# Attention and a leaky-ReLU feed-forward on one core: order of the last half products, copies of the last range on ScalarE, and no stores by GpSimd

## The chip, the core and the metric

The kernel runs on one core of a Trainium2 chip. A core has TensorE (PE in the profile, with its weight loads as PEld), VectorE (DVE), ScalarE (ACT), GpSimd (POOL) and SyncE (SP), which all run their own instruction streams and wait for one another by semaphores, and 16 DMA engines. The metric is the device time of one execution in microseconds; 387.52 us is the median of three executions of the kernel before (387.19 to 387.84).

## The reference

Softmax attention over 8 batches, 12 heads, 448 positions and 64 values per head, then a feed-forward with leaky ReLU over the 3584 tokens:

```
scores = scale * np.matmul(q, k.transpose(0, 1, 3, 2))
attn = np.exp(scores - max) ; attn = attn / (sum(attn) + 1e-09)
x = np.matmul(attn, v).transpose(0, 2, 1, 3).reshape(3584, 768)
h = x @ w_in                      # 768 -> 2048
g = np.maximum(0.01 * h, h)
return (g @ w_out).astype(np.float32)   # 2048 -> 768
```

## The kernel before

The 3584 tokens are cut into seven ranges (`cuts`); all but the first (640) and the sixth (384) have 512 tokens. After the attention of the first batches, the kernel handles range after range: `hidden(i)` computes the hidden values h of range i, and `second(i)` multiplies them by w_out and stores the result. Between the pieces of `second` a planner (`place`, with modelled times) puts attention work for the later ranges. In the last range no attention is left.

From the second range on, both parts use a scheme with seven products in place of eight for each 2 x 2 arrangement of blocks, at the price of extra sums and differences. In `hidden` these come from `mix_x_part` (line 500, differences of x on VectorE, made ahead of time while the preceding range's output part runs).

In the output part the four blocks of 128 tokens of a range form two pairs, and `block_pair(i, c)` treats one: c = 0, then c = 1. Its products P1 to P7 have 128 tokens, 384 output columns and eight matmuls each (line 679), issued in four pieces of two matmuls; between the pieces the generator yields. P1, P3, P5 accumulate in one PSUM bank (`b`), P2, P4, P6 in the other (`a`). `keep` (line 684) copies a bank into an output tile in SBUF, on VectorE or ScalarE; `join` (line 687, VectorE) adds a bank to what stands there. The two output tiles of a pair are `o1` and `o2`, each of 768 columns in f32, from a pool of three buffers. Lines 691 and 697 are differences of h on VectorE that later products need.

From the second range on, P7 of both pairs together is itself done with seven products of half the depth and half the columns: `deep(i)` (line 644), four matmuls of 192 columns each, here called half products 1 to 7. Half products 1, 3, 5 and 7 go to one bank, 2, 4 and 6 to another, and each is followed by an addition on VectorE (line 645) from the bank into `kept[i, 0]` or `kept[i, 1]`, the tiles o2 of the two pairs. The sums of h that deep needs are made at line 620 (`deep_sums`) and 647. Half product 4 is the first that adds to the second pair's o2, into columns that `keep(o2, left, b)` has filled from P5's bank just before. Half product 6 goes on top of half product 4's bank, half product 7 on top of half product 5's.

In the second pair the half products stand between the pieces of P5 (`fifth`) and P6 (`sixth`): half products 1, 2 and 3 behind the first three pieces of P5; 4, 5 and 6 behind the first three pieces of P6; 7 at the end. In the last range P6 of the second pair is split into two products of 192 columns, each with its own addition (line 733) and store, and half product 4 stands behind the first four of P6's sixteen matmuls, 5 and 6 behind the third and the last four.

`store` (line 399) writes a tile to HBM in two transfers, since 128 tokens touch two strips of the output. All go out on SyncE's queue, except in the last range, where some go out on ScalarE's, and the two of `kept[6, 0]`'s left half on GpSimd's. A store on SyncE or ScalarE waits for its addition and for the transfer that last used its completion semaphore. Line 1230 is the end of the program, where the engines drain and meet.

Of the kernel before, what the change touches and what calls it, by code (L numbers as in the profile page):

```python
# [9 lines left out]
F32 = mybir.dt.float32  # L10
# [6 lines left out]
def kernel(  # L17
# [9 lines left out]
    nc = tc.nc  # L27

    B, H, S, D = q.shape
    DM, DF = moe_w_in.shape  # L30
    P = 128
# [5 lines left out]
    NW = DM // 2  # L37
# [4 lines left out]
    NR = len(cuts) - 1  # L42
# [16 lines left out]
    o_pool = ctx.enter_context(tc.tile_pool(name="o", bufs=3))  # L59
# [9 lines left out]
    def next_slot():  # L69

        slots.append(slots.pop(0))
        return slots[-1]
# [17 lines left out]
    e_all = exp_pool.tile([P, NE, EL + EP], BF16, name="e")  # L90
# [22 lines left out]
    w_out_sb = w_pool.tile([P, MD, DM], BF16)  # L113
    MH = MD // 2
    w_mix = w_pool.tile([P, 3, MH, NW], BF16)
    QH, QW = MH // 2, NW // 2
    deep_mix = w_pool.tile([P, 3, QH, QW], BF16)
    KEEP = 4
    h = h_pool.tile([P, MD, (KEEP + 1) * P], BF16, name="h")
# [270 lines left out]
    def store(o, t0, cols=slice(0, DM), queues=(nc.sync, nc.sync)):  # L390

        queues = list(queues)
        done = 0
        while done < P:
            b, j = divmod(t0 + done, S)
            so, p = divmod(j, SC)
            n = min(SC - p, P - done)
            dst = out[b * S:(b + 1) * S].rearrange("(p so) n -> so p n", so=NSC)
            queues.pop(0).dma_start(out=dst[so, p:p + n, cols], in_=o[done:done + n, cols])  # L399
            done += n  # L400
# [102 lines left out]
    def spots(i):  # L503

        if i == 0:
            return 0, [(0, 1), (2, 3)]
        return 0, [(0, 2), (1, 3)] if cuts[i + 1] - cuts[i] == 4 * P else [(0, 1), (KEEP, 2)]

    def token(i, x):

        return KEEP * P if x == KEEP else cuts[i] + x * P
# [96 lines left out]
    kept = {}  # L608
# [14 lines left out]
    def deep(i):  # L623

        one, two = (ts(x[1], P) for x in spots(i)[1])
        lo, hi = slice(MH, MH + QH), slice(MH + QH, MD)
        s3, s1 = h_mix[:, :QH, 0], h_mix[:, QH:, 0]
        t, (t2, t3, t4) = w_mix[:, 2], (deep_mix[:, x] for x in range(3))
        left, right = slice(0, QW), slice(QW, NW)
        o = [kept[i, c] for c in range(2)]  # L630
        end = i + 1 == NR
        taken = [slots.pop(0) for _ in range(2)]
        b, a = (x[:, 0, :QW] for x in taken)
        for ps, first, x, w, c, cols in (
            (b, True, h[:, lo, one], t[:, :QH, left], 0, left),
            (a, True, h[:, hi, one], t[:, QH:, left], 0, left),
            (b, False, s1, t2, 0, right),
            (a, True, h[:, lo, two], t[:, :QH, right], 1, right),
            (b, False, s3, t3, 1, right),
            (a, False, h[:, hi, one], t[:, QH:, right], 0, right),  # L640
            (b, False, h[:, hi, two], t4, 1, left),
        ):
            for m in range(QH):
                nc.tensor.matmul(ps, x[:, m], w[:, m], start=(first and m == 0), stop=(m == QH - 1), skip_group_check=True)  # L644
            nc.vector.tensor_add(o[c][:, cols], o[c][:, cols], ps)  # L645
            if ps is a and first and c == 0:
                nc.vector.tensor_sub(h[:, hi, one], h[:, hi, one], s1)
            t0 = token(i, spots(i)[1][c][1])
            if ps is a and not first:
                store(o[0], t0, slice(0, NW) if end else slice(0, DM), (nc.gpsimd, nc.gpsimd) if end else (nc.sync, nc.sync))  # L650
            if end and c == 1 and ps is b:
                store(o[1], t0, cols, (nc.sync, nc.scalar))
            yield
        if not end:
            store(o[1], token(i, spots(i)[1][1][1]))
        slots.extend(taken)
        for x in taken:
            model["free"][id(x)] = model["now"] + 1.2

    def block_pair(i, c):  # L660

        lo, hi = slice(0, MH), slice(MH, MD)
        x1, x2 = spots(i)[1][c]
        one, two = ts(x1, P), ts(x2, P)
        s3 = h_mix[:, :, c]
        t2, t3, t4 = (w_mix[:, x] for x in range(3))
        t1 = w_out_sb[:, lo, NW:]
        left, right = slice(0, NW), slice(NW, DM)
        o1 = o_pool.tile([P, DM], F32, name="o")
        o2 = kept[i, c] = o_pool.tile([P, DM], F32, name="o")  # L670
        b, a = banks
        t0 = token(i, x2)
        last = t0 + P == B * S

        def product(ps, x, w, first=False, cols=slice(0, NW)):
            for m in range(MH):
                if m in (2, 4, 6):
                    yield
                nc.tensor.matmul(  # L679
                    ps[:, cols], x[:, m], w[:, m], start=(first and m == 0), stop=(m == MH - 1), skip_group_check=True,  # L680
                )

        def keep(o, at, ps, by=nc.vector.tensor_copy):
            by(o[:, at], ps[:, :NW])  # L684

        def join(o, at, ps):
            nc.vector.tensor_add(o[:, at], o[:, at], ps[:, :NW])  # L687

        yield
        yield from product(b, h[:, lo, one], w_out_sb[:, lo, left], first=True)  # L690
        nc.vector.tensor_sub(h[:, lo, one], h[:, lo, two], h[:, lo, one])
        short = cuts[i + 1] - cuts[i] < 4 * P
        keep(o1, left, b, nc.scalar.copy if c == 0 and (short or i + 1 == NR) else nc.vector.tensor_copy)
        yield
        yield from product(a, h[:, hi, one], w_out_sb[:, hi, left], first=True)
        join(o1, left, a)
        nc.vector.tensor_sub(h[:, hi, one], h[:, hi, one], h[:, lo, one])
        yield
        yield from product(b, h[:, lo, one], t2)
        keep(o1, right, b)  # L700
        yield
        yield from product(a, h[:, lo, two], t1, first=True)
        keep(o2, right, a)
        yield

        def fifth():
            yield from product(b, s3, t3)
            join(o2, right, b)
            if i:
                keep(o2, left, b, nc.scalar.copy if c else nc.vector.tensor_copy)  # L710
                if last:
                    store(o1, token(i, x1), left)
                    store(o2, t0, right, (nc.sync, nc.scalar))
                elif i + 1 == NR:
                    store(o2, t0, right)

        def sixth():
            if not last:
                yield from product(a, h[:, hi, one], w_out_sb[:, hi, right])
                join(o1, right, a)  # L720
                store(o1, token(i, x1))
                return
            for x in range(2):
                cols = ts(x, QW)
                for m in range(MH):
                    if m == QH or x and m == 0:
                        yield
                    nc.tensor.matmul(
                        a[:, cols], h[:, hi, one][:, m], w_out_sb[:, hi, right][:, m, cols], start=False, stop=(m == MH - 1),
                        skip_group_check=True,  # L730
                    )
                at = slice(NW + x * QW, NW + (x + 1) * QW)
                nc.vector.tensor_add(o1[:, at], o1[:, at], a[:, cols])
                store(o1, token(i, x1), at, (nc.sync, nc.scalar))

        if i and c:
            more = deep(i)
            for x, _ in enumerate(fifth()):
                yield
                next(more)  # L740
                yield
            yield
            for x, _ in enumerate(sixth()):
                yield
                if not last or x != 1:
                    next(more)
                    yield
            yield
            for _ in more:
                yield  # L750
            return
        yield from fifth()
        yield
        sums = deep_sums(i) if i else ()
        for _ in sixth():
            next(sums, None) if i else None
            yield
        if i:
            return
        yield  # L760
        yield from product(b, h[:, hi, two], t4)
        keep(o2, left, b)
        store(o2, t0)
        banks.reverse()
# [140 lines left out]
    idle = next_slot()  # L905
    slots.pop()
    a, b = idle[:, 0], idle[:, 1]
# [327 lines left out]
```

## Time and profile before

| | |
|---|---|
| median of three executions | 387.52 us |
| profiled execution: time, and span from first to last instruction | 389.63 us, 387.8 us |
| granted TensorE clock | 0.995 |
| busy: TensorE, VectorE, ScalarE, GpSimd | 96%, 64%, 66%, 47% |
| HBM read and written | 45.61 MB, 11.01 MB |

Rows of the timeline show start, length, engine, line of the kernel, operation, output<-input and how many instructions are merged, and in brackets the idle time of the engine ahead of it and what ended that. TensorE's rows overlap: a matmul's result is finished after the next one has been issued, so the distance between starts is what one costs. An engine name with a q (SPq) is its instruction queue, which issues and waits. Times are microseconds from the start of the span.

### The profile page before, as it was taken

The page shows a single profiled execution, that of the slowest core. Times are in us where ns is not written, and L with a number is a line of the kernel's source. Part 1 is how long each engine was busy: PE and PEld are TensorE (multiplying, and loading weights), DVE is VectorE, ACT ScalarE, POOL GpSimd, SP SyncE. Part 2 cuts the span into 40 slices and gives each one's busy share as a digit, 9 for nine tenths or more (in the row PEclk, how much of TensorE's full clock was granted, in tenths as well). Part 3 has the DMA queues.
Part 4 walks back from the last instruction along what each step waited for, and adds up shares of the span by engine and source line. Part 5 has one row for each costly group of instructions (what it writes and reads, how often), then busy time and mean ns, then how long its engine had stood idle before and what let it go on. Part 6 is the DMA issues. An engine that isn't in the chain of part 4 may idle for free.

```text
span 387.8 us, 10131 instructions
## 1 busy us (share of the span) xinstructions
PE 372.3 (96%) x4016; PEld 265.9 (69%) x4016; DVE 247.3 (64%) x551; ACT 257.8 (66%) x397; POOL 181.6 (47%) x378
## 2 busy tenths in 40 slices
PE   7899999989999999999999999999999999999992
PEld 3565657756598556986569865688666986688762
DVE  4763838455766867666666666666666675775772
ACT  5998885764858875488764887647876488338400
POOL 8998720977969656741558405584045100000001
PEclk9999999999999999999999999999999999999998
DMA  9999999799999759891599914999148600330022
GB/s 156 200 201 204 167 174 197 88 144 216 152 118 188 101 119 177 168 125 29 107 150 206 125 27 88 162 201 138 27 88 148 164 2 12 80 111 13 1 83 82
DMA packets 99536, 47.85 MB, mean 123 GB/s; under 512 B 63728, under 2 KB 96240, under 8 KB 99488
## 3 DMA queue, kind: packets, MB, share of 16 engines
q0 software_dynamic: 40464, 22.67, 47.6%
q1 hardware_dynamic: 58448, 24.07, 32.4%
q8 instruction: 31, 0.51, 0.5%
q10 hardware_dynamic: 576, 0.47, 0.4%
q14 instruction: 17, 0.14, 0.1%
HBM read 45.61 MB, written 11.01 MB: 146 GB/s over the span
## 4 chain that ended last, share of the span: by engine, by line
PE 72%; DMA 15%; DVE 6%; issue 3%; POOL 2%; ACT 1%; POOLq 0%; DVEq 0%; ACTq 0%
PE g L679 23%; PE g L553 13%; PE sc L553 13%; DMA fk<-in_k_dram 11%; PE sc L319 6%; PE sc L347 6%; DMA qkT<-qkb 2%; PE sc L340 2%; DMA w_in_mix<-in_k_dram 2%; PE sc L316 2%; PE sc L644 2%; DVE o L645 2%; PE g L359 1%; PE g L777 1%; PE sc L359 1%
## 5 line engine op out<-in xcount | busy, mean ns | idle before, releaser
L328 ACT ACTIVATE e<-sc 128x896 bf16<-128x896 f32 (+1 forms) x144 | 123.5, 921 | 35.6 <-PE sc L319 20.8
L679 PE MATMUL g<-w_out_sb,h 128*128 128x384 bf16 x408 | 80.7, 326 | 0.2 <-DVE o L687 0.2
L679 PEld LDWEIGHTS <-h 128*128 128x128 bf16 x520 | 48.3, 98 | 36.9 <-issue 10.0
L186 POOL COPY qkb<-fq 112x512 bf16<-112x512 bf16 x36 | 23.9, 665 | 92.7 <-DMA qkT<-qkb 73.4
L542 ACT ACTIVATE h<-c 128x512 bf16<-128x512 f32 (+1 forms) x72 | 43.5, 611 | 24.8 <-DVE c L568 15.4
L553 PEld LDWEIGHTS <-w_in_sb 128*128 128x128 bf16 x576 | 54.3, 98 | 5.3
L553 PEld LDWEIGHTS <-w_in_mix 128*128 128x128 bf16 x432 | 41.2, 98 | 4.1
L976 DVE RECIPROCAL rec<-sc 112x8 f32<-112x8 f32 x42 | 8.7, 207 | 43.4 <-PE sc L347 22.5
L399 POOL DMA_DIRECT2D out_dram<-o x2 | 1.1, 546 | 73.7 <-DVE o L645 73.7
L347 PE MATMUL sc<-v,e 128*128 128x65 bf16 x720 | 33.3, 193 | 0.0
L319 PE MATMUL sc<-qkT 64*128 64x448 bf16 (+1 forms) x210 | 32.8, 352 | 0.0
L684 DVE COPY o<-g 128x384 f32<-128x384 f32 x44 | 24.3, 552 | 12.2 <-PE g L679 11.8
L347 PEld LDWEIGHTS <-e 128*128 128x128 bf16 x720 | 31.1, 98 | 1.3
L977 DVE TENSOR_TENSOR x<-sc,rec 112x512 bf16<-112x512 f32 x42 | 29.0, 691 | 1.7 <-DVE rec L976 0.2
L687 DVE TENSOR_TENSOR o<-o,g 128x384 f32<-128x384 f32 x38 | 20.9, 550 | 12.2 <-PE g L679 10.6
L553 PE MATMUL sc<-xT,w_in_sb 128*128 128x256 bf16 (+1 forms) x216 | 28.5, 268 | 0.0
L553 PE MATMUL g<-xT,w_in_sb 128*128 128x256 bf16 (+1 forms) x216 | 28.5, 268 | 0.0
L340 PE MATMUL sc<-v,e 128*128 128x130 bf16 x120 | 26.5, 221 | 0.0
L684 ACT COPY o<-g 128x384 f32<-128x384 f32 x8 | 3.8, 478 | 33.2 <-DVE o L687 27.0
L679 PE MATMUL g<-w_mix,hmix 128*128 128x384 bf16 x104 | 23.0, 327 | 0.0
L316 PE MATMUL sc<-qkT 64*128 64x448 bf16 x144 | 19.5, 354 | 3.3 <-DMA qkT<-qkb 1.4
L159 POOL DMA_DIRECT2D fv<-in_v_dram x33 | 20.6, 631 | 4.1 <-POOL v L199 2.4
(144 smaller groups left out, 770.4 us busy)
## 6 DMA issues: line engine op xcount, KB each, us to landing
fq<-in_q_dram POOLq DMA_DIRECT2D x18, 224.0 KB, 6.2
w_in_sb<-in_moe_w_in_dram POOLq DMA_DIRECT2D x4, 768.0 KB, 10.8
w_out_sb<-in_moe_w_out_dram POOLq DMA_DIRECT2D x4, 768.0 KB, 20.4
out_dram<-o SPq DMA_DIRECT2D x7, 336.0 KB, 3.4
out_dram<-o SPq DMA_DIRECT2D x7, 288.0 KB, 2.7
fk<-in_k_dram POOLq DMA_DIRECT2D x15, 128.0 KB, 6.1
fv<-in_v_dram POOLq DMA_DIRECT2D x15, 128.0 KB, 5.8
out_dram<-o SPq DMA_DIRECT2D x7, 240.0 KB, 4.2
```

What stands on the lines that cost most here:

```text
L186: by(t[:SC, x].rearrange("p so h d -> p h so d"), f)
L316: nc.tensor.matmul(ps[:, j, :S], t[p, S + c * SC:S + c * SC + P], t[p, :S], start=True, stop=True)
L319: nc.tensor.matmul(ps[:, j, :S].rearrange("p (so s) -> p so s", so=NSC), t[p, 1, c], t[p, 0, :, :SC], start=True, stop=True,)
L328: nc.scalar.activation(e[:, :, c, :], ps[:n, :, :S], AX.Exp, scale=scale)
L340: nc.tensor.matmul(ps, e[:, EM + qc * SC:EM + qc * SC + P], vt[:, 2 * KC:].rearrange("p j d -> p (j d)"), start=True, stop=False, skip_gro ...
L347: nc.tensor.matmul(ps[:, j * (D + 1):(j + 1) * (D + 1)], e[:, at:at + P], vt[:, j * KC + c], start=False, stop=(c == KC - 1), skip_group_c ...
L542: nc.scalar.activation(hs[:, m:m + 2, cols], x.rearrange("p (m t) -> p m t", m=2), AX.Prelu, alpha=0.01)
L553: nc.tensor.matmul(ps[:, j * nh:(j + 1) * nh], w[:, kk, ts(j, P)], x[:, kk], start=(first and j == 0 and kk == 0), stop=(kk == KH - 1), sk ...
L679: nc.tensor.matmul(ps[:, cols], x[:, m], w[:, m], start=(first and m == 0), stop=(m == MH - 1), skip_group_check=True,)
L684: by(o[:, at], ps[:, :NW])
L687: nc.vector.tensor_add(o[:, at], o[:, at], ps[:, :NW])
L977: nc.vector.tensor_mul(x, ps[:, :, :, :D], rec.to_broadcast([SC, 2, 2 * NP, D]))
```

## The change

The half products are moved: in the second pair of each range from the second on but the last, half product 4 comes behind the second piece of P6 instead of the first, 5 behind the third, and 6 and 7 after all of P6. In `fifth`, the copy of P5's bank into the left half of o2 now stands ahead of the join of that bank, and VectorE does it for both pairs (before, ScalarE did it for the second pair, behind the join). In the last range P6 of the second pair is one product of 384 columns with one join and one store in two transfers; half product 4 comes behind its first piece, 5 behind its third, 6 and 7 after it. In that range the copies of P1, P3 and P4 are ScalarE's (before, only P1's of the first pair), the second pair's tiles o1 and o2 are parts of the attention buffer `e_all` instead of pool buffers, and the stores of `kept[6, 0]`'s left half go out on SyncE and ScalarE instead of GpSimd.

```
@@ deep
             if ps is a and not first:
-                store(o[0], t0, slice(0, NW) if end else slice(0, DM), (nc.gpsimd, nc.gpsimd) if end else (nc.sync, nc.sync))
+                store(o[0], t0, slice(0, NW) if end else slice(0, DM), (nc.sync, nc.scalar if end else nc.sync))
@@ block_pair
-        o1 = o_pool.tile([P, DM], F32, name="o")
-        o2 = kept[i, c] = o_pool.tile([P, DM], F32, name="o")
+        if i + 1 == NR and c:
+            o1, o2 = (e_all[:, x, :2 * DM].bitcast(F32) for x in range(2))
+        else:
+            o1, o2 = (o_pool.tile([P, DM], F32, name="o") for _ in range(2))
+        kept[i, c] = o2
...
+        idle = nc.scalar.copy
+        calm = idle if i + 1 == NR else nc.vector.tensor_copy
...
-        keep(o1, left, b, nc.scalar.copy if c == 0 and (short or i + 1 == NR) else nc.vector.tensor_copy)
+        keep(o1, left, b, idle if c == 0 and short else calm)
...
-        keep(o1, right, b)
+        keep(o1, right, b, calm)
...
-        keep(o2, right, a)
+        keep(o2, right, a, calm)
...
         def fifth():
             yield from product(b, s3, t3)
+            if i:
+                keep(o2, left, b)
             join(o2, right, b)
             if i:
-                keep(o2, left, b, nc.scalar.copy if c else nc.vector.tensor_copy)
                 if last:
...
         def sixth():
-            if not last:
-                yield from product(a, h[:, hi, one], w_out_sb[:, hi, right])
-                join(o1, right, a)
-                store(o1, token(i, x1))
-                return
-            for x in range(2):
-                cols = ts(x, QW)
-                for m in range(MH):
-                    if m == QH or x and m == 0:
-                        yield
-                    nc.tensor.matmul(
-                        a[:, cols], h[:, hi, one][:, m], w_out_sb[:, hi, right][:, m, cols], start=False, stop=(m == MH - 1),
-                        skip_group_check=True,
-                    )
-                at = slice(NW + x * QW, NW + (x + 1) * QW)
-                nc.vector.tensor_add(o1[:, at], o1[:, at], a[:, cols])
-                store(o1, token(i, x1), at, (nc.sync, nc.scalar))
+            yield from product(a, h[:, hi, one], w_out_sb[:, hi, right])
+            join(o1, right, a)
+            store(o1, token(i, x1), right if last else slice(0, DM), (nc.sync, nc.scalar if last else nc.sync))

         if i and c:
             more = deep(i)
-            for x, _ in enumerate(fifth()):
+            for _ in fifth():
                 yield
                 next(more)
                 yield
             yield
             for x, _ in enumerate(sixth()):
                 yield
-                if not last or x != 1:
+                if x != int(last):
                     next(more)
                     yield
-            yield
             for _ in more:
                 yield
             return
```

The attention work that the planner puts between the pieces stands at the same places in the changed program.

## The prediction

> **What bounds the kernel now.** I read the busy shares first, then a table by stage, then the waits, then the places where TensorE (PE) waits, and last the end of the program.
>
> ```profile
> PE 372.3 (96%) x4016; PEld 265.9 (69%) x4016; DVE 247.3 (64%) x551; ACT 257.8 (66%) x397; POOL 181.6 (47%) x378
> ```
>
> ```profile
> 362.50:382.20 19.70, 18.24 (x132) 12.06 (x130) 14.00 (x31) 1.93 (x4) 0.06 (x1) 1.00 0.20 57
> 382.20:387.80 5.60, 0.00 (x0) 0.00 (x0) 0.00 (x0) 0.00 (x0) 1.01 (x2) 0.68 0.28 85
> ```
>
> The columns are window, length, then busy time of PE, PEld, VectorE (DVE), ScalarE (ACT) and GpSimd (POOL), granted clock, DMA share, GB/s. Over the whole run TensorE is busy 96%. In the output part of the last range (362.5 to 382.2) it loses 1.5 us, and then 5.6 us pass with no arithmetic at all. TensorE therefore sets the time up to about 382, and whatever ends last after it sets the rest.
>
> ```profile
> DVE o L645 <- ACT o L684: 2.4, 5, 0.6
> PE sc L644 <- DVE o L645: 2.4, 4, 0.9
> SPq L1230 <- PEq L1230: 2.1, 2, 1.6
> ```
>
> These rows of the table of waits (who <- for whom: total, times, longest) name the two places the change touches: a chain ScalarE copy -> VectorE addition -> sixth half product, and a wait of SyncE's queue at the closing line 1230. Below, "half products" 1 to 7 are those of the function deep, P1 to P7 those of the pair, and "middle ranges" are the five from the second to the sixth.
>
> **Middle ranges: what is removed and what comes instead.** PE, VectorE and ScalarE rows of the third range (202 to 205 us), then of the second (153 to 156), then of the sixth (341 to 344):
>
> ```profile
> 202.20 0.54 DVE L687 TENSOR_TENSOR o<-o,g 128x384 f32<-128x384 f32 x1
> ...
> 202.66 0.49 PE L679 MATMUL g<-w_out_sb,h 128*128 128x384 bf16 x2
> 202.82 0.48 ACT L684 COPY o<-g 128x384 f32<-128x384 f32 x1 [2.50 <-issue]
> 203.34 0.81 DVE L645 TENSOR_TENSOR o<-o,sc 128x192 f32<-128x192 f32 x2 [0.59 <-ACT o L684]
> 203.74 0.49 PE L644 MATMUL sc<-w_mix,h 128*128 128x192 bf16 x4 [0.59 <-DVE o L645]
> ...
> 204.39 0.49 PE L644 MATMUL sc<-deep_mix,h 128*128 128x192 bf16 x4
> ...
> 204.72 0.49 PE L553 MATMUL g<-xT,w_in_sb 128*128 128x256 bf16 x3
> ```
>
> ```profile
> 153.84 0.68 DVE L500 TENSOR_TENSOR x_mix<-xT 128x512 bf16<-128x512 bf16 x1
> 154.50 0.35 DVE L645 TENSOR_TENSOR o<-o,sc 128x192 f32<-128x192 f32 x1
> ...
> 155.11 0.35 DVE L645 TENSOR_TENSOR o<-o,sc 128x192 f32<-128x192 f32 x1
> ```
>
> ```profile
> 155.89 0.82 PE L553 MATMUL g<-xT,w_in_sb 128*128 128x256 bf16 x6
> ```
>
> ```profile
> 341.49 0.55 DVE L687 TENSOR_TENSOR o<-o,g 128x384 f32<-128x384 f32 x1
> 341.96 0.42 DVE L500 TENSOR_TENSOR x_mix<-xT 128x512 bf16<-128x512 bf16 x1
> 342.59 0.35 DVE L645 TENSOR_TENSOR o<-o,sc 128x192 f32<-128x192 f32 x1 [0.21 <-ACT o L684]
> 342.86 0.42 DVE L500 TENSOR_TENSOR xT<-xT 128x512 bf16<-128x512 bf16 x1
> 343.20 0.35 DVE L645 TENSOR_TENSOR o<-o,sc 128x192 f32<-128x192 f32 x1
> ```
>
> ```profile
> 342.60 0.49 PE L679 MATMUL g<-w_out_sb,h 128*128 128x384 bf16 x2
> ...
> 343.98 0.82 PE L553 MATMUL g<-xT,w_in_sb 128*128 128x256 bf16 x6
> ```
>
> Third range, before: the fifth product's sum is joined by VectorE at 202.20, copied by ScalarE at 202.82, and only then can the addition of half product 4 run (203.34), because it adds to columns that the copy writes. Half product 6 writes the bank that this addition reads, so TensorE starts it at 203.74 instead of right behind the piece at 202.66. A piece or half product takes 0.33 us of issue (204.39 to 204.72).
>
> Third range, after: VectorE copies at 202.20 and joins one step later. Two neighbouring VectorE operations of this size stand 0.47 us apart (341.49 to 341.96), so the join is at 202.67 and the addition of half product 4 at 203.14, 0.20 earlier. TensorE followed the start of that addition by 0.40 (203.34 to 203.74, 0.05 behind its end), so half product 6 starts at 203.54. All four pieces of P6 now stand ahead of it, so only one half product follows it, not a piece and a half product. The addition of half product 5, 0.46 behind that of 4 (0.81 for the two less 0.35), ends at 203.95 and frees the bank of half product 7, which starts at 204.00 and ends its issue at 204.33, against 204.72 before: a gain of 0.39. The addition may also have to wait for the whole join (0.54 and not 0.47): then 0.3. The fourth and fifth range have the same order on VectorE; I take 0.33 for each of the three, together 1.0.
>
> Second range: there VectorE has work on x_mix (L500, 0.68) between the join and the addition, and ScalarE's copy was hidden under it. The copy on VectorE pushes everything back by 0.47: additions at 154.97 and 155.58, the latter ending at 155.93, half product 7 at 155.98, next stage at 156.31 against 155.89. A loss of 0.42. Sixth range: additions at 342.76 (one x_mix step of 0.33 behind the join) and 343.36, the latter ending at 343.71. TensorE's own order would bring half product 7 to 343.58 (342.60 plus three steps of 0.33); it starts at 343.76 and the next stage at 344.09, a loss of 0.11.
>
> Sum of the middle ranges: 1.0 - 0.42 - 0.11 = a gain of 0.4 to 0.5; I take **0.4**. Bounds: if the copy cost its whole 0.47 in the three ranges too, less the piece of 0.33 that is moved, the five would lose 0.95; if no stall were left at all, they would gain the 2.4 of the table. The nearest rows are those above, so I keep 1.0 of loss and 1.2 of gain for the range.
>
> At no cost: the changed order of copy and join in the first pair of each range (both are VectorE's already, and the last of the two ends at the same time); the stores of a middle range, two of which swap on SyncE's queue (the buffers are written again only after the next range's hidden stage, for instance 343.98 to 362.49 on TensorE); ScalarE's copy, 0.48, which nothing waits for any more. VectorE's x_mix work ends up to 0.47 later; TensorE needs it some two steps into the hidden stage, and without that cover each such stage would lose up to 0.47.
>
> **Last range: products and additions.** The same chain and a split P6:
>
> ```profile
> 378.20 0.55 DVE L687 TENSOR_TENSOR o<-o,g 128x384 f32<-128x384 f32 x1
> ...
> 378.66 0.49 PE L728 MATMUL g<-w_out_sb,h 128*128 128x192 bf16 x4
> ...
> 379.97 0.49 PE L728 MATMUL g<-w_out_sb,h 128*128 128x192 bf16 x4 [0.82 <-DVE o L733]
> ...
> 381.49 0.68 DVE L645 TENSOR_TENSOR o<-o,sc 128x192 f32<-128x192 f32 x2
> 382.14 1.08 POOL L399 DMA_DIRECT2D out_dram<-o  x2 [73.73 <-DVE o L645]
> ```
>
> P6's second half waits until its first half has been read out (379.97). After the change P6 is one product of full width, with the same TensorE time (16 matmuls of 192 columns were four steps, 8 of 384 are four). P6 begins at 378.00 (two steps of 0.33 ahead of the row at 378.66), and from there TensorE runs eight steps without that stop: half product 5 at 379.31, 6 at 379.97, 7 at 380.30, each done 0.49 after its start, the last at 380.79. On VectorE: copy 378.20, join 378.67, additions of 4 at 379.14 and of 5 at 379.84 (when half product 5 is done), join of P6 at 380.17, additions of 6 at 380.64 and of 7 at 380.97, ending at 381.32 against 382.17: **0.85 earlier**. The copies moved to ScalarE (five in the two pairs) take 0.48 there, as at 202.82, and each has one product into the other bank, four steps or 1.3 us, to hide under; without that cover TensorE would stop up to 0.5 each time. New waits: the joins of this range wait for ScalarE's copies, which end some 0.8 ahead of them (1.3 less 0.48); behind a join stand the sums of h and the additions, for which TensorE waits. The two output tiles taken from the attention buffers are free: their last readers ran at 335.
>
> ```profile
> L340 PE MATMUL sc<-v,e x120: 219/220/231, 107.7 to 335.2; 128*128 128x130 bf16 x120
> ```
>
> **Last range: stores and the end.**
>
> ```profile
> 381.72 0.88 ACTq L399 DMA_DIRECT2D out_dram<-o  x2
> ```
>
> ```profile
> L1230 SPq EVENT_SEMAPHORE  x11: 17/28/28, 385.0 to 387.8; - x11
> ...
> L1230 POOLq DRAIN  x3: 46/102/4437, 382.6 to 387.6; - x3
> L1230 SPq DRAIN  x3: 7/7/7, 385.6 to 387.3; - x3
> ```
>
> ```profile
> out_dram<-o ACTq DMA_DIRECT2D x1, 168.0 KB, 2.3
> out_dram<-o ACTq DMA_DIRECT2D x2, 84.0 KB, 2.0
> out_dram<-o SPq DMA_DIRECT2D x1, 144.0 KB, 2.7
> ...
> out_dram<-o POOLq DMA_DIRECT2D x1, 144.0 KB, 2.4
> ```
>
> The closing code (line 1230; columns: count, shortest/median/longest in ns, first and last start) shows what stands at the end. GpSimd issues its second store at about 382.7 (two in 1.08 from 382.14) and it lands 2.3 to 2.4 later, at 385.0, where SyncE's last waits go through; at 385.6 they are done. Then SyncE stands 1.6 more (the longest wait in its row above), and the only thing still running is GpSimd's drain: 4.44 us from 382.6, to 387.0. The common end takes 0.8 from there.
>
> After the change GpSimd's last work is in the attention, so its drain is over early. The final stores go out on SyncE and ScalarE; of each queue's last three, the first follows P6's join (380.72), and an issue takes some 0.45 (0.88 for two in the ScalarE row above), so the last goes out near 381.7, landing 2.0 to 2.3 later, 383.8 (with the 2.7 of the 144 KB row 384.4). SyncE's waits that are still open then cost 0 to 0.6, the common end 0.8: 384.6 to 385.8, I take 385.0. Against 387.8: **2.8 earlier**, of which 1.4 is the drain, 1.2 the earlier landing. Bounds 1.9 and 3.2.
>
> A page of the Trainium skill speaks against this: "DMA: Bandwidth & Descriptors", section "Issuing engines are not separate DMA queues", says all issuers run on the same 16 engines and several issuers only save issue time. By that rule giving up GpSimd's queue saves nothing and costs issue time, and the sum would be that of the rival "the end does not move" below. The rows agree with the rule for the transfer (2.4 us against 2.0 to 2.7), but show a drain besides that this section does not mention.
>
> **Sum.** 2.8 + 0.4 = 3.2 us inside the span. The profiled execution took 389.63 (span 387.8 and 1.8 around it), so 386.4; the median of the unprofiled runs, 387.52, lies 2.1 below it, and less 3.2 gives **384.3**.
>
> **Rivals.** *The end does not move* (the drain is there whoever issued the last store, or costs nothing unprofiled): only the earlier additions, 0.85, and the middle 0.4 remain: 386.3. For it: one execution alone shows the drain. Against: it begins at 382.6, with GpSimd's last issue, ahead of which GpSimd stood idle for 73.73 us.
> *The middle ranges lose* because VectorE is late everywhere as in the second range: 5 x 0.42 = 2.1 lost, and the end gains 2.8: 386.8. For it: VectorE runs without idle time there. Against: it stood 2.4 us in all waiting for ScalarE, 0.59 in the third range, more than the copy's 0.47.
> *The last stores queue up* on two queues and the end is later than now: in the compiled program each such store reuses one of eight completion counters and waits until the store that had it has landed. ScalarE's last one takes the counter of the 168 KB store issued behind P5's join, near 379.25; with 2.3 to landing that is 381.55, just ahead of 381.7. It decides once that landing takes over 2.45 us, and makes the kernel slower once it takes over 5.65 (3.2 more); at 7 us the time is 384.3 + 4.55 = 388.9. For it: landings of up to 9.5 us occur among the stores of this run, as the row below says. Against: the same store took 2.3.
>
> ```profile
> DMA to landing us min/median/max: 1.5/2.9/9.5
> ```
>
> **How the numbers follow.** Forecast 0.75, the end does not move 0.10, the middle loses 0.10, stores queue up 0.05. The range takes the forecast with its bounds: 3.2 + 0.8 at best (383.5) and, with the end at its lower bound and the middle at zero, 385.6; I extend it to 385.9 toward the two middling rivals. A difference under 0.2% (0.8 us) can't be told from no change. Forecast and first rival are faster; the second lies on the border with 0.7 gained, and half of it is counted as the same; the third is mostly slower: faster 0.90, same 0.06, slower 0.04.
>
> **What would show it.** Right: GpSimd has no row in the last 70 us and its drain at the closing line is short; SyncE's closing waits begin before 384.6 on the scale of the old profile; no ScalarE releaser of L645; half product 6 in the third to fifth range starts within 0.3 of the piece before it; the second range's next stage comes later than 155.89. Wrong: a GpSimd or other drain of microseconds after the last landing; PE idle of over 0.5 before half product 6 or 7 in most ranges; the last landing over 3 us behind the last addition.

## The result, and the profile after

| | before | after |
|---|---|---|
| median of the runs | 387.68 us (387.19 to 387.90, 4 runs) | 384.70 us (384.23 to 384.87, 4 runs) |
| profiled execution | 389.63 us | 384.23 us |
| its span | 387.8 us | 382.4 us |

The 384.23 of the changed kernel is one of its four runs; the 389.63 is not among the four of the kernel before. The ratio of the times is 0.9923, with a 95% interval from 0.9906 to 0.9940. The kernel is 3.0 us faster. The forecast was 384.3 us, with a range from 383.5 to 385.9.

**By stage.** First the busy shares of the page of the changed kernel, then two windows of its table by stage, with the columns of the prediction's windows (PE, PEld, DVE, ACT, POOL, clock, DMA share, GB/s). The first has the length of the output window shown before, the second goes from the last addition to the end.

```profile
PE 371.8 (97%) x4008; PEld 265.4 (69%) x4008; DVE 247.6 (65%) x551; ACT 257.3 (67%) x396; POOL 182.2 (48%) x376
```

```profile
359.30:379.00 19.70, 18.09 (x125) 11.53 (x122) 11.52 (x26) 3.88 (x8) 0.00 (x0) 1.00 0.23 62
378.07:382.40 4.33, 0.00 (x0) 0.00 (x0) 0.00 (x0) 0.00 (x0) 0.00 (x0) 0.75 0.43 131
```

GpSimd has no work left in either window, and the stretch without arithmetic is 4.3 us instead of 5.6. VectorE has given work to ScalarE in the last range: 11.52 against 14.00, and 3.88 against 1.93.

**By place.** I split the gain of the span into pieces, each measured between the same two events of both traces. A middle range goes from the start of half product 1 to the first product of the next stage; the stretches between these pieces agree within 0.02 us.

| piece | before | after | change |
|---|---|---|---|
| up to half product 1 of the second range | 150.25 | 147.79 | -2.46 |
| second range | 5.64 | 5.98 | +0.34 |
| third, fourth, fifth range | 5.34, 5.29, 5.13 | 4.93, 4.93, 4.76 | -0.41, -0.36, -0.37 |
| sixth range | 4.66 | 4.76 | +0.10 |
| last range, half product 1 to the end of the last addition | 6.14 | 5.21 | -0.93 |
| last addition to the end of the span | 5.66 | 4.38 | -1.28 |

The first piece is not the change. Up to there the two programs are the same, and the kernel of the experiment e1_pool_stores_only, which is the kernel before up to the last range, reaches the same product at 148.05. All profiles of this study have it between 147.6 and 150.8; the changed kernel profiled a second time has it at 148.36. So the profiled execution of before had a late start, some 2 us. A changed kernel can have it too: e9_small_pool_copy is at 150.76. The chain that ended last on its page, and then that of after, agree (shares of the span by engine):

```profile
PE 72%; DMA 15%; DVE 6%; issue 3%; POOL 2%; ACT 1%; POOLq 0%; DVEq 0%; ACTq 0%
```

```profile
PE 89%; DVE 5%; issue 2%; DMA 1%; ACT 1%; POOL 0%; DVEq 0%; POOLq 0%; ACTq 0%
```

In the late start the chain goes back through transfers (15%, and 13% in e9_small_pool_copy), in the other it hardly does (1%). The remaining pieces sum to 0.70 + 0.93 + 1.28 = 2.91 us, beside 2.98 between the medians: 0.7 from the middle ranges, 2.2 from the last range and the end.

**Third range after.** VectorE and TensorE rows of the changed kernel:

```profile
200.08 0.55 DVE L687 COPY o<-g 128x384 f32<-128x384 f32 x1
200.55 0.54 DVE L693 TENSOR_TENSOR o<-o,g 128x384 f32<-128x384 f32 x1
200.86 0.49 PE L682 MATMUL g<-w_out_sb,h 128*128 128x384 bf16 x2
201.01 0.80 DVE L645 TENSOR_TENSOR o<-o,sc 128x192 f32<-128x192 f32 x2
201.41 0.49 PE L644 MATMUL sc<-w_mix,h 128*128 128x192 bf16 x4
201.86 0.49 PE L644 MATMUL sc<-deep_mix,h 128*128 128x192 bf16 x4
202.19 0.49 PE L553 MATMUL g<-xT,w_in_sb 128*128 128x256 bf16 x3
```

Copy, join, additions stand 0.47 and 0.46 apart, as forecast, and none waits for ScalarE. Half product 6 starts 0.55 behind the last piece of P6, where the free step is 0.33, and half product 7 another 0.45 later: TensorE still loses 0.22 and 0.12 here. Both stops follow VectorE by the 0.40 of before (201.01 to 201.41).

**Second range after.** VectorE rows and then the TensorE rows of the two half products that wait:

```profile
150.91 0.55 DVE L687 COPY o<-g 128x384 f32<-128x384 f32 x1
151.37 0.54 DVE L693 TENSOR_TENSOR o<-o,g 128x384 f32<-128x384 f32 x1
151.83 0.41 DVE L500 TENSOR_TENSOR x_mix<-xT 128x512 bf16<-128x512 bf16 x1
152.17 0.34 DVE L645 TENSOR_TENSOR o<-o,sc 128x192 f32<-128x192 f32 x1
152.43 0.69 DVE L500 TENSOR_TENSOR x_mix<-xT,x_mix 128x512 bf16<-128x512 bf16 x1
153.04 0.34 DVE L645 TENSOR_TENSOR o<-o,sc 128x192 f32<-128x192 f32 x1
```

```profile
152.57 0.49 PE L644 MATMUL sc<-w_mix,h 128*128 128x192 bf16 x4 [0.69 <-DVE o L645]
153.44 0.49 PE L644 MATMUL sc<-deep_mix,h 128*128 128x192 bf16 x4 [0.38 <-DVE o L645]
```

Here the x_mix work stands between join and additions, VectorE runs without a gap, and the copy that it now has pushes TensorE back: 1.07 us of stops in these two rows.

**The end after.** From a timeline of the changed kernel, issues of stores included, then the closing line 1222 (1230 before), then issues with the size of a store and the time to landing:

```profile
376.07 1.81 SPq L399 DMA_DIRECT2D out_dram<-e  x3
376.08 1.87 ACTq L399 DMA_DIRECT2D out_dram<-e  x3
...
377.72 0.35 DVE L645 TENSOR_TENSOR e<-e,sc 128x192 f32<-128x192 f32 x1
377.98 0.38 SPq L399 DMA_DIRECT2D out_dram<-o  x1
378.33 0.32 ACTq L399 DMA_DIRECT2D out_dram<-o  x1
378.44 0.38 SPq L399 DMA_DIRECT2D out_dram<-e  x1
378.75 0.40 ACTq L399 DMA_DIRECT2D out_dram<-e  x1
```

```profile
L1222 SPq EVENT_SEMAPHORE  x11: 17/28/28, 378.9 to 382.4; - x11
...
L1222 POOLq DRAIN  x3: 51/102/4109, 304.7 to 382.2; - x3
L1222 SPq DRAIN  x3: 7/7/13, 381.6 to 381.9; - x3
```

```profile
out_dram<-e ACTq DMA_DIRECT2D x1, 120.0 KB, 2.4
```

GpSimd's drain is still 4.11 us long, but it begins at 304.7, at GpSimd's last work in the attention, and is over 70 us before the end. The last addition ends at 378.07; ScalarE issues the last store at 378.75, 0.68 later, and 2.4 later it lands, at 381.15. That is 3.08 behind the addition; before, the last landing was 2.85 behind it. From the last landing to the end of the span it is 1.30 us, where it was 2.81. ScalarE's store of the other tile went out 0.35 after SyncE's half of it (378.33 against 377.98), and the last one is behind it on the same queue.

### The profile page after: what moved, and what is told of

Read it like the earlier page. It is cut to its first block, busy times and chain, and to the rows that moved or that the text cites. A ratio compares the mean times of both kernels' runs of the same rounds, so it can differ in the third digit from the quotient of the medians.

```text
span 382.4 us, 10102 instructions
## 1 busy us (share of the span) xinstructions
PE 371.8 (97%) x4008; PEld 265.4 (69%) x4008; DVE 247.6 (65%) x551; ACT 257.3 (67%) x396; POOL 182.2 (48%) x376
## 4 chain that ended last, share of the span: by engine, by line
PE 89%; DVE 5%; issue 2%; DMA 1%; ACT 1%; POOL 0%; DVEq 0%; POOLq 0%; ACTq 0%
PE g L682 25%; PE g L553 14%; PE sc L553 14%; PE sc L319 7%; PE sc L347 6%; PE g L421 4%; PE sc L316 4%; PE sc L359 3%; PE g L769 3%; PE sc L644 2%; PE g L810 2%; PE sc L340 2%; DMA w_in_mix<-in_q_dram 1%; PE g L359 1%; PE g L298 1%
## 5 line engine op out<-in xcount | busy, mean ns | idle before, releaser
L682 PE MATMUL g<-w_out_sb,h 128*128 128x384 bf16 x416 | 81.7, 326 | 0.2 <-DVE o L693 0.2
L682 PEld LDWEIGHTS <-h 128*128 128x128 bf16 x528 | 49.1, 98 | 37.5 <-issue 9.6
L565 ACT COPY c<-g 128x512 f32<-128x512 f32 (+1 forms) x12 | 6.8, 569 | 32.0 <-PE g L553 32.0
L693 DVE TENSOR_TENSOR o<-o,g 128x384 f32<-128x384 f32 x36 | 19.7, 548 | 5.4 <-PE g L682 4.8
L159 POOL DMA_DIRECT2D fk<-in_k_dram x33 | 20.9, 645 | 1.4 <-DMA fv<-in_v_dram 1.4
L359 PEld LDWEIGHTS <-e 112*128 112x128 bf16 x432 | 20.0, 98 | 2.1 <-issue 0.7
```

The lines of the kernel that those rows point to most:

```text
L159: nc.gpsimd.dma_start(out=t[p, :n, :, :so].rearrange("p u h so d -> p (u h) (so d)"), in_=(q, k, v)[x][b, hs, keys].rearrange("h (p so) d ...
L359: nc.tensor.matmul(ps[:, qc, :], t[:SC, at:at + P], vt[:, c], start=(c == 0), stop=(c == NSC - 1),)
L682: nc.tensor.matmul(ps[:, cols], x[:, m], w[:, m], start=(first and m == 0), stop=(m == MH - 1), skip_group_check=True,)
```

## The experiments

The kernels were run in three groups, each against runs of the kernel before on the same chip (medians 387.59, 387.97 and 388.29); the ratios are taken within a group, while medians of different groups compare only to about the 0.7 us by which these differ. "The end" is the time from the last addition to the end of the span.

**Only the stores leave GpSimd (e1_pool_stores_only)**, in the kernel before:

```
-                store(o[0], t0, slice(0, NW) if end else slice(0, DM), (nc.gpsimd, nc.gpsimd) if end else (nc.sync, nc.sync))
+                store(o[0], t0, slice(0, NW) if end else slice(0, DM), (nc.sync, nc.scalar if end else nc.sync))
```

> The kernel before, with only the two last GpSimd stores given to SyncE and ScalarE. Theory (GpSimd's drain of about 4.1 to 4.4 us starts when its last work is done, and ends the program as long as that work is a store at the end): from the end of the last VectorE addition to the end of the span 5.66 us before, now 4.2 to 4.5, so about 1.3 us less, 386.4 against 387.7. Rival (the end does not move): 387.7, and 5.6 from the last addition to the end.

Measured: 385.77 us, ratio 0.9953 (0.9941 to 0.9964), so 1.8 us by this line alone, more than the 1.3 expected. The end is 4.01 us against 5.66. The last landing is 2.85 behind the last addition, the same as in the kernel before, so no part of this gain is an earlier landing. Closing line of this kernel:

```profile
L1230 POOLq DRAIN  x3: 46/102/4110, 305.8 to 383.7; - x3
L1230 SPq DRAIN  x3: 7/7/7, 383.2 to 383.5; - x3
```

The drain has moved to 305.8, and the median went with it.

**The whole change but for those stores (e2_after_with_pool)**: the same line the other way round, in the changed kernel.

> The changed kernel with those two stores back on GpSimd. Theory: from the last addition to the end 5.6 to 5.8 us where the changed kernel has 4.38, so 1.2 to 1.4 slower, about 386.0. Rival (the gain comes from the earlier additions and the middle ranges alone): 384.7.

Measured: 386.08 us, ratio 0.9964 (0.9951 to 0.9978), 1.4 above the changed kernel's 384.70 (1.6 by the ratios). The end is 5.88, though the last landing is only 0.08 later, 3.16 behind the last addition. Closing line:

```profile
L1222 POOLq DRAIN  x3: 46/102/4587, 378.6 to 383.7; - x3
L1222 SPq DRAIN  x3: 7/7/13, 381.9 to 383.5; - x3
```

The drain begins behind GpSimd's second store, ends at 383.2 (378.6 + 4.59) and is what SyncE's closing waits for. Of the 3.0 us, 1.4 to 1.8 belong to these two stores.

**Any late work of GpSimd (e9_small_pool_copy)**: the changed kernel, with a copy of one column into an unused tile behind the last addition; nothing is stored by GpSimd.

```
+        if end:
+            nc.gpsimd.tensor_copy(gate[:, :1], o[1][:, :1])
```

> The changed kernel with one GpSimd copy of a single column (from the last output tile into a scratch tile nothing reads) behind the last addition. If the drain comes with any late GpSimd work: it starts some 0.3 us behind the last addition and lasts 4.1 to 4.4, so the span ends 5.1 to 5.5 behind the last addition where it was 4.38: 0.7 to 1.1 slower, about 385.6. Rival (the drain is long only because GpSimd waits for its own late stores): the copy's drain is short and the time stays at 384.7.

Measured: 385.36 us, ratio 0.9952 (0.9934 to 0.9970). Last additions, the copy, and the closing line (1224 here):

```profile
380.57 0.35 DVE L645 TENSOR_TENSOR e<-e,sc 128x192 f32<-128x192 f32 x1
381.08 0.19 POOL L655 COPY gate<-e 128x1 f32<-128x1 f32 x1 [73.10 <-DVE e L645]
...
L1224 POOLq DRAIN  x3: 46/102/3883, 381.1 to 385.5; - x3
L1224 SPq DRAIN  x3: 7/7/7, 384.5 to 385.2; - x3
```

A copy of 0.19 us is followed by a drain of 3.88 and the end is 4.81, 0.43 longer. The expected 5.1 to 5.5 was too much, because the drain was shorter than 4.44; but the rival, that the drain is long only where GpSimd has stores of its own in flight, falls by this trace. The medians alone don't show the cost: the interval overlaps that of the changed kernel (0.9906 to 0.9940).

**A store by GpSimd that is early enough (e8_pool_store_early)**: the changed kernel, with the left 192 columns of half product 2's tile stored by GpSimd right behind their last addition (the closing store then carries the other columns only).

```
-                store(o[0], t0, slice(0, NW) if end else slice(0, DM), (nc.sync, nc.scalar if end else nc.sync))
+                store(o[0], t0, right if end else slice(0, DM), (nc.sync, nc.scalar if end else nc.sync))
+            if end and ps is a and first and c == 0:
+                store(o[0], t0, left, (nc.gpsimd, nc.gpsimd))
```

> The changed kernel with the first 192 columns of the first pair's tile stored early as in the run with the early store, but by GpSimd, some 3 us ahead of the last addition. If only the moment of GpSimd's last work counts: a drain of 4.1 to 4.6 us starts near 375, ends near 380, ahead of the last landing, and the end is that of the run with the early store, 3.9 behind the last addition. Rival (a store on GpSimd in the output part costs the end in any case): 4.4 or more.

Measured: 384.42 us, ratio 0.9899 (0.9878 to 0.9920). The issues and the closing line:

```profile
375.14 1.08 POOL L399 DMA_DIRECT2D out_dram<-o  x2 [69.57 <-DVE o L645]
...
L1224 POOLq DRAIN  x3: 46/102/4435, 375.6 to 382.6; - x3
L1224 SPq DRAIN  x3: 7/7/12, 382.0 to 382.3; - x3
```

The drain, 4.44 long, is over at 380.0, ahead of SyncE's 382.0, and costs nothing. The end, 4.34, is no shorter than the changed kernel's 4.38; 3.9 was expected. The last landing is still 3.05 behind the last addition, and why the smaller closing store did not land earlier here stays open.

**The same early store by SyncE and ScalarE (e6_quarter_early)**: `(nc.sync, nc.scalar)` in the last line of the diff above.

> The changed kernel with the first 192 columns of the first pair's tile stored right behind half product 2, where they are complete, so that only 192 columns remain behind half product 6. If the last landing is late because of what is in flight at the end (480 KB in the last three pairs of stores): the last landing comes 0.3 to 0.5 earlier, 384.3. Rival (the last landing is bound by the issue and the fixed 2 us of the very last store): no change beyond 0.1, 384.6 to 384.7.

Measured: 384.65 us, ratio 0.9918 (0.9904 to 0.9931). In the profile the end is 3.92, 0.46 shorter, with the landing 2.76 behind the addition, 0.3 earlier as expected; in the median no difference can be told from the changed kernel.

**Only the order of the half products in the middle ranges (e3_order_only)**, in the kernel before:

```
-                if not last or x != 1:
+                if x != int(last):
...
-            yield
+            if last:
+                yield
```

> The kernel before, with only the half products of the middle ranges moved (4 and 5 one piece later, 6 and 7 behind P6); the copy stays on ScalarE behind the join. From the start of half product 1 to the next stage the five middle ranges take 5.64, 5.34, 5.29, 5.13, 4.66 us before and 5.98, 4.93, 4.93, 4.76, 4.76 changed. By the steps of the prediction the addition of 4 keeps its time, and half product 7 waits for that of 5: 5.59, 5.14, 5.10, 4.93, 4.60, a gain of 0.7 in all. Rival (moving a piece ahead of the stall changes nothing, because the half products wait for the additions anyway): as before.

Measured: 387.13 us, ratio 0.9975 (0.9956 to 0.9994). The five middle ranges take 5.83, 5.10, 5.10, 4.93, 4.60, in sum 25.56 against 26.06: a gain of 0.50 where 0.7 was expected, the difference being the second range (5.83 where 5.59 was expected).

**Only VectorE's copy (e4_copy_only)**, in the kernel before:

```
+            ahead = i and i + 1 < NR
+            if ahead:
+                keep(o2, left, b)
...
-                keep(o2, left, b, nc.scalar.copy if c else nc.vector.tensor_copy)
+                if not ahead:
+                    keep(o2, left, b, nc.scalar.copy if c else nc.vector.tensor_copy)
```

> The kernel before, with only the copy of the middle ranges made by VectorE ahead of the join; the order of the half products stays. By the steps of the prediction the additions of 4 and 5 come 0.2 earlier in the third to fifth range and 0.47 later in the second, 0.17 later in the sixth: 6.1, 5.14, 5.10, 4.93, 4.8 from half product 1 to the next stage, a loss of 0.0 to 0.1 in all. Rival (the copy on VectorE is what gains, the order does not matter): 5.98, 4.93, 4.93, 4.76, 4.76 as in the changed kernel.

Measured: 387.50 us, ratio 0.9990 (0.9973 to 1.0008), no change that can be told. The ranges take 5.99, 5.13, 5.12, 4.96, 4.82, in sum 26.02. TensorE in the third range, first of e3_order_only, then of e4_copy_only:

```profile
201.94 0.49 PE L644 MATMUL sc<-w_mix,h 128*128 128x192 bf16 x4 [0.22 <-DVE o L645]
202.40 0.49 PE L644 MATMUL sc<-deep_mix,h 128*128 128x192 bf16 x4
```

```profile
202.03 0.49 PE L644 MATMUL sc<-w_mix,h 128*128 128x192 bf16 x4 [0.38 <-DVE o L645]
202.36 0.49 PE L679 MATMUL g<-w_out_sb,h 128*128 128x384 bf16 x2
```

The order shortens the stop from 0.59 to 0.22, because a piece of P6 fills it. The copy shortens it to 0.38 and costs about as much in the second and sixth range (+0.35 and +0.16) as it brings in the other three (0.55). In these three the order alone brings 0.63 and both together 1.14, so there each of the two pays. Over all five ranges both bring 0.70, where the order alone has 0.50 and the copy alone 0.04; the second range, which differs among the profiles (see the last section), is too uncertain to say more of that difference.

**The copy of the second pair by ScalarE, but ahead of the join (e5_scalar_ahead)**, in the changed kernel:

```
-                keep(o2, left, b)
+                keep(o2, left, b, idle if c and i + 1 < NR else nc.vector.tensor_copy)
```

> The changed kernel, but in the middle ranges the second pair's copy is ScalarE's again, now ahead of the join. ScalarE is free when P5 ends, so VectorE only joins and adds. If the changed kernel's losses come from the copy's 0.47 in VectorE's queue: 5.6, 4.6, 4.6, 4.6, 4.6 us from half product 1 to the next stage, 1.3 less in all, about 383.4. Rival (a join behind a ScalarE copy waits again, as before): 5.4 to 5.0 in the third to fifth range, 385.3.

Measured: 383.16 us, ratio 0.9874 (0.9854 to 0.9894), below the changed kernel's interval (0.9906 to 0.9940). The ranges take 5.58, 4.58, 4.59, 4.58, 4.81, in sum 24.14 against its 25.36, 1.2 less. The end is shorter too, 4.04 against 4.38: here ScalarE's store behind half product 6 is not late (377.72, SyncE's half at 377.65). Third range of this kernel:

```profile
199.77 0.48 ACT L687 COPY o<-g 128x384 f32<-128x384 f32 x1 [1.23 <-PE g L682]
200.43 0.54 DVE L693 TENSOR_TENSOR o<-o,g 128x384 f32<-128x384 f32 x1
200.89 0.34 DVE L645 TENSOR_TENSOR o<-o,sc 128x192 f32<-128x192 f32 x1
201.21 0.49 PE L682 MATMUL g<-w_out_sb,h 128*128 128x384 bf16 x2
201.53 0.49 PE L644 MATMUL sc<-w_mix,h 128*128 128x192 bf16 x4
201.86 0.49 PE L644 MATMUL sc<-deep_mix,h 128*128 128x192 bf16 x4
```

TensorE goes in steps of 0.33 without a stop. What cost time before was that ScalarE's copy came behind the join, not that ScalarE made it.

**Both additions (e7_both)**: the edits of e5_scalar_ahead and e6_quarter_early together.

> The changed kernel with both: the middle copies by ScalarE ahead of the join, and the first 192 columns of the first pair's tile of the last range stored early. The two touch different stages, so their gains should add: 1.3 and what the early store alone gives.

Measured: 382.91 us, ratio 0.9870 (0.9850 to 0.9890), the lowest median; the end is 3.83, and ScalarE's store is not late here either (378.42 and 378.35). Beside e5_scalar_ahead the early store's share can't be told from nothing.

**Which queue's store is late (e10_swap_queues)**: the changed kernel, with the halves of the store behind P5's join given to the other queue each.

```
-                    store(o2, t0, right, (nc.sync, nc.scalar))
+                    store(o2, t0, right, (nc.scalar, nc.sync))
```

> The changed kernel with one store's two transfers exchanged: of the second pair's right half (behind P5's join) SyncE takes the 168 KB transfer and ScalarE the 24 KB one. In the changed kernel ScalarE's store behind half product 6 goes out 0.36 us after SyncE's, 2.26 behind its own 168 KB store, about when that one lands; so do those of the runs with the same queues. If it waits for that landing: here it goes out beside SyncE's (within 0.05), ScalarE's last store some 0.3 earlier, last landing 2.7 to 2.8 behind the last addition instead of 3.07, 0.3 less in all. Rival (the fourth store of a queue is late whatever went before it, or the transfers are bound by the 480 KB in flight): last landing at 3.0 to 3.1, no change.

Measured: 384.70 us, ratio 0.9909 (0.9890 to 0.9928); the end is 4.19. ScalarE's later store still goes out at 378.36 against SyncE's 378.02, again 2.25 behind the stores of P5's join. So it is not the size of ScalarE's own earlier transfer that holds it. The last landing is 2.91 behind the last addition, between the expected 2.7 to 2.8 and the rival's 3.0 to 3.1.

**All three edits (e11_all_three)**, those of e7_both and e10_swap_queues.

> The changed kernel with the middle copies by ScalarE ahead of the join, the early store of the first 192 columns and the exchanged transfers. If the third adds to the other two: from the last addition to the end 3.5 to 3.6 where the two alone have 3.83, about 382.7. Rival: as the two alone, 382.9.

Measured: 383.07 us, ratio 0.9866 (0.9845 to 0.9888), the end 3.75. Here ScalarE's store is not late (377.92 against 377.85), and the landing is 2.58 behind the addition; but ScalarE's store is not late in e5_scalar_ahead and e7_both either, without the exchange, so the exchange isn't shown to do it. For the end 3.5 to 3.6 was expected. The time can't be told from that of e7_both.

**The changed kernel once more (c1_after_again):**

> The changed kernel once more, for its own spread: from half product 1 to the next stage 5.98, 4.93, 4.93, 4.76, 4.76 in its first profile, 4.38 from the last addition to the end, half product 1 of the second range at 147.8 where the profile of before has 150.3. If that start is a matter of the execution and not of the change, it can lie anywhere from 147.6 to 150.8 again; the median stays at 384.7 within 0.3.

Measured: 384.95 us, ratio 0.9915 (0.9897 to 0.9932). The ranges take 6.07, 4.94, 4.93, 4.76, 4.76 and the end 4.35, so these pieces repeat within 0.1 us of the first profile; only the start of the program does not (148.36 here).

## Why the prediction was right, and where its sizes were off

**Right: the bound.** TensorE sets the time up to the last addition, and GpSimd's drain and the last landing set the rest. Moving the two stores alone gave 1.8 us, and giving them back cost 1.4 (e1_pool_stores_only, e2_after_with_pool). The rival "the end does not move" fell with them: it would have left 386.3. So did the sum that the prediction drew from the Trainium skill, "DMA: Bandwidth & Descriptors", section "Issuing engines are not separate DMA queues", by which all issuers run on the same 16 DMA engines and several of them save only issue time. For the transfers the traces agree: the two stores landed 2.3 and 2.4 us after GpSimd issued them, and 2.6 and 2.5 after SyncE and ScalarE did. But the issuer made 1.4 to 1.8 us of difference to the whole, through the drain.

**Right: the middle ranges.** Forecast were +0.42 for the second range, -0.33 for each of the three and +0.11 for the sixth; measured +0.34, -0.41, -0.36, -0.37 and +0.10. The addition stood 0.46 behind the join, so the 0.39 of the detailed working held, and the wait for the whole join (0.54), for which it was cut to 0.33, did not come. The sum is 0.7 instead of 0.4. How near the second range came is partly luck, since its loss lies between 0.07 and 0.45 among the eight kernels with VectorE's copy. The rival "the middle ranges lose" saw the second range rightly and was wrong in holding it for the rule. What the sum did not separate are the two edits: the order of the half products gains by itself, while the copy on VectorE gains 0.55 in three ranges, loses 0.51 in the other two and about breaks even. The prediction's upper bound for these ranges, a gain of 1.2, was too low for what they hold: e5_scalar_ahead gains 1.9 against the kernel before.

**Right: the products and additions of the last range.** 0.85 was forecast, 0.93 measured; half product 7 came 4.25 behind half product 1, where the working had 4.27.

**Too large: the end.** The term "2.8 earlier" for end and additions measured 2.2. The step that failed is the last landing, put 2.5 us behind the last addition (383.8 against 381.32) and measured at 3.08. Of that, 0.3 is the issue of ScalarE's last store (0.68 behind the addition, not 0.4, by the pause described under the third rival), the rest its time to landing (2.4, where 2.0 to 2.3 was taken). So the landing came 0.7 earlier in the program instead of 1.2. The drain's term was right: 1.4 was forecast for it, and from the last landing to the end 1.5 went. (The prediction's 1.4 and 1.2 make 2.6; it does not say where the other 0.2 of its 2.8 comes from, and its lower bound, 385.8 against 387.8, is 2.0 and not 1.9.) "The last landing over 3 us behind the last addition" was one of the signs named for being wrong, and it came.

**Third rival.** It said that ScalarE's last store would wait for the 168 KB store to land. It does use that store's completion counter, but the landing is at 378.40 and ScalarE's queue reaches this wait only at 378.70. What made it late is a pause ahead of another store: ScalarE's half behind half product 6 goes out 0.35 us after SyncE's. That it stands 2.25 behind the stores of P5's join looks like a wait for a landing, and is none: the completion counter of this store was last used by one that landed at 372.56, the stores of P5's join landed at 377.96 and 378.40, neither at 378.33, and the addition that it needs had already released SyncE's half at 377.98. If ScalarE's instructions are counted, a pause of 0.32 to 0.33 stands ahead of the 576th in eight traces (both of the changed kernel, and those of e2, e3, e6, e8, e9 and e10), whether that is a store or the wait ahead of one, and a transfer of 8 KB on the instruction queue q14 begins 0.7 to 1.1 us behind it. In e5_scalar_ahead, e7_both and e11_all_three the last such transfer begins at 361.6 to 362.3, long ahead of the stores, and no store is late. So the pause goes with a place in ScalarE's instruction stream and not with the stores; that it comes from loading instructions fits, but no run isolates it.

**Wrong, and without effect on the median: the profiled time.** 386.4 was forecast for the profiled execution, 384.23 came. The 2.1 us between before's profiled time and its median were carried on as if they went with profiling; they were a late start of that one execution, 2.46 us ahead of the second range. Since the forecast subtracted the change from the median, the error cancelled.

**The signs.** GpSimd has no row in the last 70 us, no addition waits for ScalarE, and half product 6 starts 0.22 behind the end of the last piece's issue in the third range, within the 0.3 that was said. "Its drain at the closing line is short" was wrong: it is as long, but early.

The two errors have opposite signs, 0.3 more in the middle and 0.6 less at the end; the sum, 3.2 against 2.9 to 3.0, owes part of its closeness to that. The range, 383.5 to 385.9, was narrower than the bounds it named: 3.2 and 1.2 together give 383.1, and 1.9 less a loss of 1.0 gives 386.6.

## What to carry to other kernels

At the end of a program look at what each engine's closing code stands on: the last use of an engine can cost more than the work it does there, and e8_pool_store_early shows that the same use some 3 us earlier costs nothing: its drain began 2.9 us ahead of the last addition, that of e2_after_with_pool 0.5 behind it. Where a copy and a join read the same bank and something waits for both, put the copy first and give it to the engine that is free then (e5_scalar_ahead); taking it over on the busy engine only moves the wait. And compare two profiles piece by piece from a common event, since their starts can differ by more than the change does.

## What the runs showed of the hardware that was not expected

GpSimd's drain at the closing line takes 3.9 to 4.6 us whatever came before it: 4.44 and 4.59 behind stores, 4.11 behind its last attention work at 304.7, and 3.88 behind a copy of one column.

VectorE's difference of 128x512 (L500) has two durations. The rows of the second range after show them: 0.41 at 151.83 and 0.69 at 152.43. GpSimd's rows of the changed kernel at that time:

```profile
152.23 0.61 POOL L186 COPY qkb<-fq 112x512 bf16<-112x512 bf16 x1 [4.58 <-DMA qkT<-qkb]
152.79 0.70 POOL L190 COPY qkb<-fk 128x384 bf16<-128x384 bf16 x1
```

The long one runs beside these copies, the short one ahead of them. In c1_after_again, the same program, the first of the two differences meets this copy and is the long one:

```profile
152.41 0.72 DVE L500 TENSOR_TENSOR x_mix<-xT 128x512 bf16<-128x512 bf16 x1
```

```profile
152.35 0.50 POOL L190 COPY qkb<-fk 128x384 bf16<-128x384 bf16 x1
```

So it is not the operands. In the fourteen traces together none of the 219 such differences without a GpSimd copy beside them took over 0.43 us; of the 61 with one, ten took 0.57 to 0.75 and most of the others 0.42. So in these traces the long one always has a copy beside it, and a copy beside it is not enough. The Trainium skill, "SBUF — State Buffer", section "🔬 SBUF: two separate sides", says that VectorE and GpSimd share a pair of ports under an exclusive lock; the traces agree in direction, and the size here is 0.28 us on 0.41; which of the copies take the lock, no run shows. The second range took 5.71 to 6.09 us among the kernels with VectorE's copy, which may come from how many differences meet a copy; no run isolates it.
